# Retention and routed experts on one core: scatters of slots placed between a block's key and query scalings, seven routing groups, and logits block by block

## The chip, the cores and the metric

The kernel runs on one core of a Trainium2 chip. A core has five engines that run side by side: TensorE (PE in the profile, its weight loads PEld), VectorE (DVE), ScalarE (ACT), GpSimd (POOL) and SyncE (SP), and 16 DMA engines. The metric is the device time of one execution in microseconds (us); the median of several runs counts.

## The reference

The first half is a decaying linear attention over 4 sequences of 768 steps with 8 heads of 64. Its output is 3072 rows of 512. The second half sends each row to one of 8 experts, the one whose direction it points to most.

```
state = gamma * state + outer(k[t], v[t])        # per batch and head
x[t]  = scale * q[t] @ state                     # rows x: 3072 x 512
xn, en = x / (|x| + 1e-6), emb / (|emb| + 1e-6)
logits = xn @ en.T / tau                         # 3072 x 8
expert = argmax(logits);  gate = softmax(logits)[expert]
out[row] = gate * (relu(x[row] @ w1[expert]) @ w2[expert])
```

## The kernel before

The attention is done in 12 blocks m = 0 to 11 of 256 time steps, three to a sequence, all heads at once (loop at L773). Time inside a block is handled with products of 128 steps: keys are multiplied by gamma^-t and queries by gamma^t (scale_k L341, scale_q L334, two GpSimd instructions of 128x512 each per block), both are transposed on TensorE (L350, L368) and copied out of PSUM by ScalarE (L355, L369), then TensorE makes the scores (L381), VectorE masks them (L401), and TensorE multiplies them with the values (intra, L445) and adds the part that comes from the running state (inter, L445; the state's own products are L415). ScalarE takes the output out of the two banks py0 and py1 (take, L464 and L467). Logits of a block are one product with the experts' normalised directions (L492), which VectorE turns into rows (L500).

Blocks are scaled two ahead: in block m, GpSimd scales the keys and queries of block m+2 once the first mask of block m is done (L796 to L800, `after(..., i)`), and the transposes of block m+1 stand near the end of block m. The order of the instructions on each engine is the order in which the program is written out; nothing reorders it.

Routing goes by groups of blocks (GROUPS, L50). When a group's last block has its logits, TensorE sums them over the quarters of the features (sums, L510) and VectorE chooses the expert (choose, L520 to L530) and adds to the running counts (L548, L550). One block later TensorE counts earlier rows of the same expert (count, L537 to L541) and VectorE makes of this each row's slot in a table (ranks, L557 to L561: `sloti`). GpSimd then writes one entry per row into the table `tbl` in DRAM, by an indirect DMA for every 128 rows (place, L570): 24 of them in all, of which the first 18 are the table of the "early" rows (blocks 0 to 8). In the text a run is several such scatters one behind the other on GpSimd. In block 10 the early entries are read back (L606) and their rows gathered (L600).

In the kernel before, the scatters of block m stand behind all four scalings on GpSimd (L842): none in blocks 0 to 3, then 2, 2, 2, 3, 3, 4 in blocks 4 to 9 and the last 2 of the 18 in block 10. The directions (expert_emb, L627 to L650) are normalised in three steps at the ends of blocks 0, 1 and 2, mostly on VectorE, so logits start only in block 3, with three blocks' at once (L844). Rows of block m-1 go to DRAM with two VectorE transposes (L472) and four DMAs on SP's queue (L479); in a block with a choice they go before it, but in block 9 behind it (L857 to L870).

Behind the blocks come the experts' two layers, in which TensorE multiplies with weights split into two parts (L237, L1040, L1090). The change touches none of it.

Of the kernel before, what the change touches and what calls it, by code (L numbers as in the profile page):

```python
# [11 lines left out]
F32 = mybir.dt.float32  # L12
F32R = mybir.dt.float32r
BF16 = mybir.dt.bfloat16
FP16 = mybir.dt.float16
I32 = mybir.dt.int32
AF = mybir.ActivationFunctionType
# [7 lines left out]
P = 128  # L25
# [21 lines left out]
EROWS = ((0, P), (1, P), (2, EARLY - 2 * P))  # L47
LATE = CAPS[0] - EARLY
assert LATE == P
GROUPS = ((0, 1, 2), (3, 4, 5), (6, 7), (8,), (9, 10), (11,))  # L50
NBE = 2 * 9
SW = 16
FILL = 512
# [52 lines left out]
def retention_moe(ctx: ExitStack, tc: tile.TileContext, q, k, v, emb, tau, w1, w2, const, const16, out):  # L106
# [67 lines left out]
    def after(i, o):  # L174
        tc.add_manual_dep(i.ins, o.ins.name, SYNC, reason="pace")
# [451 lines left out]
    def expert_emb():  # L627
        em = ap_.tile([NE, DM], F32, name="parts")
        nc.scalar.dma_start(out=em, in_=emb)
        tt = cp.tile([NE, 1], F32, name="tt")  # L630
        nc.scalar.dma_start(out=tt, in_=tau.broadcast_to([NE, 1]))
        yield
        rt = cp.tile([NE, 1], F32, name="rt")
        nc.vector.reciprocal(out=rt, in_=tt)
        sq = cp.tile([P, DM], BF16, name="sq")
        es = cp.tile([NE, 1], F32, name="es")
        nc.vector.scalar_tensor_tensor(out=sq[:NE], in0=em, scalar=1.0, in1=em, op0=ALU.mult, op1=ALU.mult, accum_out=es)
        en = cp.tile([NE, 1], F32, name="en")
        steps = norm_of(en, es, NE, 1)
        next(steps)  # L640
        yield
        for _ in steps:
            pass
        nc.vector.tensor_scalar(out=em, in0=em, scalar1=en, scalar2=rt, op0=ALU.mult, op1=ALU.mult)
        yield
        ps = pt_()
        for j in range(KT):
            nc.tensor.transpose(ps[:, j * NE:(j + 1) * NE], em[:, j * P:(j + 1) * P], ident[:NE, :NE])
        nc.vector.tensor_copy(out=enT[:, :, :NE], in_=ps[:, :KT * NE].rearrange("p (j e) -> p j e", e=NE))
        yield  # L650
# [72 lines left out]
    warm = cp.tile([P, 1], F32, name="warm")  # L723
    nc.gpsimd.memset(warm, 1.0)
    nc.scalar.activation(out=warm, in_=warm, func=AF.Exp)
    make_identity(nc, ident)
    for _ in range(W0):
        nc.tensor.matmul(idle, zeros[:, :P], zeros, start=True, stop=True)
# [23 lines left out]
            turn_k(0, s, kps[s], range(2 * i, 2 * i + 2))  # L752
    copy_k(0, 0, kps[0])
    copy_k(0, 1, kps[1], nc.vector.tensor_copy)
    spread_v(0, 0)
    spread_v(0, 1)
    for s in range(2):
# [4 lines left out]

    last_of = {ms[-1]: g for g, ms in enumerate(GROUPS)}
    waiting, ready = None, []

    def place_ranks(g):
        pr = count(g)
# [5 lines left out]
    for m in range(NM):  # L773
# [8 lines left out]
        for u in range(2):  # L782
            o = masks(scores(m, u), u)
            if u == 0:
                i = o[0]
        n = 2 if m < 7 else 3 if m < 8 else 4
        if m == NM - 2:
            place(ready)
            del ready[:]
# [3 lines left out]
            nc.sync.dma_start(out=cst2, in_=const[:, _C1:])  # L793
            nc.sync.dma_start(out=tri, in_=const16)

        if m + 2 < NM:  # L796
            for s in range(2):
                after(scale_k(m + 2, s), i)
            for s in range(2):
                after(scale_q(m + 2, s), i)  # L800
        if m == 2:
            nc.gpsimd.tensor_copy(out=zt[:, :, :2].bitcast(I32), in_=C("ids").rearrange("p (n o) -> p n o", o=2))
        if m == NM - 3:
# [8 lines left out]
        if m == 0:  # L812
            state(0)
            state_copy(0)
            state_sums(0)
            intra(0, 0)
            intra(0, 1)
            transpose_k(1, 0)
# [10 lines left out]
        else:  # L829
# [9 lines left out]
                    in_=none), i)  # L839
            if waiting is not None and m < NM - 2:  # L840
                place_ranks(waiting)
            place(ready[:n])  # L842
            del ready[:n]
            for i in () if m < 3 else (0, 1, 2) if m == 3 else (m - 1,):  # L844
                logits_rows(i, logits_products(i))
            if nxt:
                state_sums(m + 1)
                spread_v(m, 1, nc.vector.tensor_copy)
                transpose_k(m + 1, 0)
                transpose_q(m + 1, 0)  # L850
                i = transpose_q(m + 1, 1)
                if m + 3 < NM:
                    after(load_v(m + 3), i)
                transpose_k(m + 1, 1)
                if m == NM - 2:
                    spread_v(m + 1, 0)
                if m == NM - 3:  # L857
                    z = sums(done)
                    run_all(choose(done, z))
                    run_all(add_counts(done))  # L860
                rows(m - 1, gathered if m == NM - 2 else None)
                if m == NM - 2:
                    for low in first:
                        low()
                    load_piece(gathered)
                    load_piece(gathered)
                if done is not None and m != NM - 3:
                    z = sums(done)
                    run_all(choose(done, z))
                    run_all(add_counts(done))  # L870
                intra(m, 0)
                intra(m, 1)
            else:
                intra(m, 0)
                z = sums(done)
                run_all(choose(done, z))
                run_all(add_counts(done))
                for low in lows:
                    low()
                intra(m, 1)  # L880
                pr = count(done)
                ps = [turn_rows(xge, EROWS, kt, bank(f"pst{kt}")) for kt in range(2)]
                run_all(ranks(done, pr))
                place(range(span(done).start, span(done).stop))
# [4 lines left out]
        if m == NM - 2:  # L889
            spread_v(m + 1, 1)  # L890
            lows = [split_cast(), split_cast()]
        if m < 3:
            next(emb_steps)
        if m == NM - 1:
            for kt in range(KT):
# [476 lines left out]
```

## Time and profile before

| what | us |
|---|---|
| median of 3 runs | 408.5 (405.87 to 409.03) |
| the profiled execution | 404.42 |
| span of its profile, first to last instruction | 402.6 |
| mean granted TensorE clock in it | 0.991 of full speed |

The page counts, for each engine, the time in which one of its instructions runs. A view of stretches cuts the span at given times; a row has start and end, the length, the busy time of PE, PEld, DVE, ACT and POOL with the number of their instructions, the granted TensorE clock as a share of full speed, the share of the DMA engines, and GB/s. The times in a timeline are from the span's start; a row ends with the idle time of its engine ahead of it and with what ended that.

### The profile page before, as it was taken

Reading aid. Unit: us, or ns where it says so; the run is one execution under the profiler, and the core shown is the slowest. Engines: PE = TensorE matmul, PEld = TensorE weight load, DVE = VectorE, ACT = ScalarE, POOL = GpSimd, SP = SyncE. Lnnn points to the kernel's source line nnn. Section 1 sums busy time; section 2 is a strip of 40 time slices with the busy share of each in tenths; the row PEclk is TensorE's granted clock in tenths of the full one; section 3 lists DMA queues with packets and bytes.
Section 4 is the critical chain, followed back from the end, with each engine's and each line's share of the span. In section 5 each row is a group of like instructions: output and inputs, shape, how many; then the busy total and the mean of one; then the engine's idle time right before and its main releaser. Section 6 shows DMA issues by size and latency. Waiting matters only on the chain.

```text
span 402.6 us, 9524 instructions
## 1 busy us (share of the span) xinstructions
PE 389.6 (97%) x3646; PEld 356.8 (89%) x3646; DVE 255.1 (63%) x539; ACT 213.4 (53%) x378; POOL 151.1 (38%) x170
## 2 busy tenths in 40 slices
PE   7999999999999999999999999999999999999992
PEld 4898888877869988999999999999889889999971
DVE  5598987667798748744861864586377446576300
ACT  4565665554784457464553845554585445453410
POOL 2677476678325252412702511340272062000131
PEclk9999999999899999999999999999999999999998
DMA  8999999888357959687878796797969887933121
GB/s 233 263 307 276 258 264 266 235 232 229 77 142 228 292 181 303 173 267 210 264 235 217 254 326 167 215 302 217 258 234 329 206 258 229 241 113 103 36 100 43
DMA packets 88479, 88.39 MB, mean 220 GB/s; under 512 B 10808, under 2 KB 67000, under 8 KB 88424
## 3 DMA queue, kind: packets, MB, share of 16 engines
q1 hardware_dynamic: 83176, 74.60, 64.9%
q0 software_dynamic: 5072, 13.03, 9.8%
q8 instruction: 30, 0.49, 0.5%
q14 instruction: 25, 0.20, 0.2%
q10 hardware_dynamic: 176, 0.07, 0.1%
HBM read 65.01 MB, written 18.79 MB: 208 GB/s over the span
## 4 chain that ended last, share of the span: by engine, by line
PE 90%; DMA 4%; issue 2%; ACT 2%; DVE 1%; SPq 1%; POOL 0%; POOLq 0%; ACTq 0%
PE pst L237 12%; PE b L237 10%; PE py L237 10%; PE py L1040 8%; PE py L445 8%; PE b L1090 6%; PE b L1040 6%; PE pst L1040 6%; PE b L381 5%; PE py L1090 4%; PE pst L415 3%; PE b L350 3%; PE pst L1090 3%; PE b L368 2%; PE b L492 1%
## 5 line engine op out<-in xcount | busy, mean ns | idle before, releaser
L224 DVE TENSOR_TENSOR wlo<-raw,whi 128x1024 fp32r<-128x1024 f32 x64 | 77.9, 1220 | 20.9 <-ACT whi L219 14.8
L1072 POOL DMA_INDIRECT out_dram<-og,si x28 | 29.1, 1038 | 126.8 <-ACT og L1065 74.9
L219 ACT CAST whi<-raw 128x1024 fp32r<-128x1024 f32 x64 | 66.2, 1043 | 3.2 <-DMA raw<-in_moe_w_dram 3.2
L1021 DVE STREAM_TRANSPOSE xt<-xg 128x384 f32<-128x384 f32 (+1 forms) x28 | 15.7, 578 | 33.6 <-DMA xg<-xs 33.5
L600 POOL DMA_INDIRECT xr<-xd,gi x24 | 29.0, 1207 | 17.2 <-DMA raw<-in_moe_w_dram 10.0
L401 DVE TENSOR_TENSOR pm<-b,mask 128x512 f32<-128x512 f32 x48 | 29.8, 681 | 8.4 <-PE b L381 8.4
L344 POOL TENSOR_TENSOR hl<-wlo,cst 128x512 f32<-128x512 f32 x22 | 22.7, 1049 | 29.9 <-DVE pm L401 13.1
L237 PE MATMUL pst<-xl,whi 128*128 128x380 f32 (+7 forms) x96 | 32.1, 335 | 0.0
L237 PE MATMUL pst<-xh,whi 128*128 128x380 f32 (+7 forms) x96 | 32.0, 334 | 0.0
L237 PE MATMUL pst<-xh,wlo 128*128 128x380 f32 (+7 forms) x96 | 32.0, 333 | 0.0
L570 POOL DMA_INDIRECT tbl<-zt,sloti x24 | 24.4, 1018 | 16.4 <-DVE sloti L561 7.3
L381 PE MATMUL b<-qT,kT 64*128 64x128 f32 x384 | 28.2, 286 | 2.4 <-DVE kT L355 0.9
L381 PEld LDWEIGHTS b<-qT,kT 64*128 64x128 f32 x384 | 24.3, 191 | 5.6 <-issue 3.3
L1022 ACT CAST xh<-xt 128x408 fp32r<-128x408 f32 (+6 forms) x28 | 14.2, 510 | 26.2 <-DVE xt L1021 25.9
L237 PE MATMUL py<-xl,whi 128*128 128x288 f32 (+7 forms) x80 | 26.3, 328 | 0.5 <-DVE xl L625 0.5
L237 PE MATMUL b<-xh,whi 128*128 128x408 f32 (+7 forms) x80 | 26.7, 334 | 0.0
L237 PE MATMUL b<-xl,whi 128*128 128x408 f32 (+7 forms) x80 | 26.7, 333 | 0.0
L237 PE MATMUL b<-xh,wlo 128*128 128x408 f32 (+7 forms) x80 | 26.6, 332 | 0.0
L237 PE MATMUL py<-xh,whi 128*128 128x288 f32 (+7 forms) x80 | 26.3, 329 | 0.0
L237 PE MATMUL py<-xh,wlo 128*128 128x288 f32 (+7 forms) x80 | 26.2, 328 | 0.0
L263 POOL TENSOR_TENSOR r<-r,half 128x4 f32<-128x4 f32 (+1 forms) x9 | 8.9, 993 | 41.7 <-DVE r L262 41.7
L445 PE MATMUL py<-pm,vs 128*64 128x128 f32 x384 | 24.5, 277 | 0.1
(222 smaller groups left out, 1032.9 us busy)
## 6 DMA issues: line engine op xcount, KB each, us to landing
raw<-in_moe_w_dram SPq DMA_DIRECT2D x60, 512.0 KB
whi<-in_q_dram SPq DMA_DIRECT2D x24, 256.0 KB
xd<-x SPq DMA_DIRECT2D x48, 128.0 KB
wlo<-in_k_dram SPq DMA_DIRECT2D x11, 512.0 KB
xs<-xr SPq DMA_DIRECT2D x6, 768.0 KB
whi<-in_v_dram SPq DMA_DIRECT2D x6, 512.0 KB
wlo<-in_v_dram SPq DMA_DIRECT2D x6, 512.0 KB
xg<-xs SPq DMA_DIRECT2D x16, 192.0 KB
```

The lines of the kernel that those rows point to most:

```text
L219: nc.scalar.copy(out=hv, in_=rv)
L224: eng.tensor_tensor(out=lv, in0=rv, in1=hv.bitcast(F32), op=ALU.subtract)
L237: nc.tensor.matmul(acc[:, :w], a[:, f], x[:, kt, cols], start=(n == 0), stop=(n == 3 * KT - 1))
L344: return eng.tensor_tensor(out=ks_r[:, m % 3, s, h], in0=kin[m % 3][:, h, s], in1=w[:, h], op=ALU.mult)
L381: nc.tensor.matmul(psc[a][:, j], kTs[m][a * D:(a + 1) * D, j, u].rearrange("p s c -> p (s c)"), q_cols(m, a, j, u), start=True, stop=True, ...
L401: o.append(nc.vector.tensor_tensor(out=pm, in0=psc[a], in1=w, op=ALU.mult))
L445: nc.tensor.matmul(pys[m][b][o * D:(o + 1) * D, j], lhsT, rhs, start=first, stop=True, skip_group_check=True)
L570: i = nc.gpsimd.indirect_dma_start(out=tbl[:, :], out_offset=bass.IndirectOffsetOnAxis(ap=sloti[:, n:n + 1], axis=0), in_=zt[:, n], in_off ...
L600: return nc.gpsimd.indirect_dma_start(out=xr[:n, j, :], out_offset=None, in_=xd[:rows_, :], in_offset=bass.IndirectOffsetOnAxis(ap=gi[:n, ...
L1040: nc.tensor.matmul(acc[:, :c], a[:, f], x[:, kt, :c], start=(n == 0), stop=(n == 3 * FT - 1))
L1072: i = nc.gpsimd.indirect_dma_start(out=out[:, :], out_offset=bass.IndirectOffsetOnAxis(ap=si[:n, e, j:j + 1], axis=0), in_=og[:n, j, :], i ...
L1090: nc.tensor.matmul(acc[:s, :], x[:, kt, at], a, start=(n == 0), stop=(n == 3 * FT - 1))
```

## The change

Seven groups instead of six, so that two groups of three become pairs and block 7 stands alone; the number of scatters per block comes from a table. On GpSimd a block's order becomes: two key scalings, scatters, two query scalings. In a block that also makes ranks (4, 6, 8, 9) one query scaling stands ahead of the scatters. In block 0 all four scalings of block 2 stand behind the steps of the directions. The directions' squares move from VectorE to ScalarE, the scaling of `emb` from VectorE to GpSimd, and the whole chain into the head and block 0. Logits are made in every block from block 1 on, one block's at a time. The choice of a group stands ahead of the rows' transposes in every block. The scatters per block become 2, 3, 2, 3, 2, 4 in blocks 4 to 9, and again 2 in block 10.

```diff
-GROUPS = ((0, 1, 2), (3, 4, 5), (6, 7), (8,), (9, 10), (11,))
+GROUPS = ((0, 1, 2), (3, 4), (5, 6), (7,), (8,), (9, 10), (11,))
+PLACES = {4: 2, 5: 3, 6: 2, 7: 3, 8: 2, 9: 4}
...
         nc.scalar.dma_start(out=tt, in_=tau.broadcast_to([NE, 1]))
         yield
+        sq = cp.tile([P, DM], BF16, name="sq")
+        es = cp.tile([NE, 1], F32, name="es")
+        nc.scalar.activation(out=sq[:NE], in_=em, func=AF.Square, accum_out=es)
+        yield
         rt = cp.tile([NE, 1], F32, name="rt")
         nc.vector.reciprocal(out=rt, in_=tt)
-        sq = cp.tile([P, DM], BF16, name="sq")
-        es = cp.tile([NE, 1], F32, name="es")
-        nc.vector.scalar_tensor_tensor(out=sq[:NE], in0=em, scalar=1.0, in1=em, op0=ALU.mult, op1=ALU.mult, accum_out=es)
...
-        nc.vector.tensor_scalar(out=em, in0=em, scalar1=en, scalar2=rt, op0=ALU.mult, op1=ALU.mult)
+        nc.gpsimd.tensor_scalar(out=em, in0=em, scalar1=en, scalar2=rt, op0=ALU.mult, op1=ALU.mult)
...
     nc.scalar.activation(out=warm, in_=warm, func=AF.Exp)
+    next(emb_steps)
...
     copy_k(0, 1, kps[1], nc.vector.tensor_copy)
+    next(emb_steps)
...
+    def scale_ahead(m, i, what=(scale_k, scale_q), ss=range(2)):
+        if m + 2 < NM:
+            for f in what:
+                for s in ss:
+                    after(f(m + 2, s), i)
...
-        n = 2 if m < 7 else 3 if m < 8 else 4
...
-        if m + 2 < NM:
-            for s in range(2):
-                after(scale_k(m + 2, s), i)
-            for s in range(2):
-                after(scale_q(m + 2, s), i)
+        if m:
+            scale_ahead(m, i, (scale_k,))
+        masked = i
...
             state_sums(0)
+            next(emb_steps)
+            scale_ahead(0, i)
...
             if waiting is not None and m < NM - 2:
                 place_ranks(waiting)
+                scale_ahead(m, masked, (scale_q,), (0,))
+            n = PLACES.get(m, 0)
             place(ready[:n])
             del ready[:n]
-            for i in () if m < 3 else (0, 1, 2) if m == 3 else (m - 1,):
-                logits_rows(i, logits_products(i))
+            scale_ahead(m, masked, (scale_q,), range(waiting is not None and m < NM - 2, 2))
+            logits_rows(m - 1, logits_products(m - 1))
...
-                if m == NM - 3:
+                if done is not None:
                     z = sums(done)
                     run_all(choose(done, z))
                     run_all(add_counts(done))
                 rows(m - 1, gathered if m == NM - 2 else None)
...
-                if done is not None and m != NM - 3:
-                    z = sums(done)
-                    run_all(choose(done, z))
-                    run_all(add_counts(done))
...
-        if m < 3:
+        if m == 0:
             next(emb_steps)
```

## Rows read from the trace of the kernel before

**Rows 1.** The page: the span and part 1.
```profile
span 402.6 us, 9524 instructions
PE 389.6 (97%) x3646; PEld 356.8 (89%) x3646; DVE 255.1 (63%) x539; ACT 213.4 (53%) x378; POOL 151.1 (38%) x170
```
**Rows 2.** Stretches from one block's first score to the next's, blocks 3 to 10.
```profile
34.38:43.34 8.96, 8.96 (x195) 7.61 (x193) 7.09 (x16) 4.66 (x9) 4.70 (x6) 1.00 1.02 293
43.34:52.14 8.80, 8.79 (x161) 7.59 (x159) 7.88 (x19) 5.67 (x10) 5.31 (x5) 1.00 0.92 256
52.14:60.71 8.57, 8.54 (x187) 7.36 (x185) 6.59 (x12) 5.47 (x10) 6.50 (x8) 1.00 0.90 253
60.71:69.22 8.51, 8.16 (x178) 7.09 (x176) 6.52 (x14) 4.89 (x9) 6.54 (x7) 1.00 0.93 258
69.22:78.46 9.24, 9.00 (x162) 7.80 (x160) 7.58 (x19) 5.11 (x9) 6.23 (x8) 1.00 0.86 241
78.46:87.87 9.41, 9.28 (x195) 7.88 (x193) 6.19 (x14) 5.49 (x10) 7.05 (x7) 1.00 0.81 230
87.87:98.16 10.29, 9.42 (x188) 7.90 (x186) 7.13 (x24) 5.48 (x10) 7.26 (x8) 1.00 0.89 229
98.16:110.89 12.73, 11.58 (x153) 9.61 (x153) 8.38 (x20) 8.01 (x13) 5.32 (x6) 0.87 0.46 112
```
**Rows 3.** The chain that ended last: start, us, what; blocks 3 and 5.
```profile
37.96 1.43 PE b L492 x24
...
41.29 0.22 PE b L510 x8
...
56.16 0.57 PE b L492 x8
```
**Rows 4.** Timeline of POOL: scatters of blocks 5, 8, 8 and 9.
```profile
60.38 0.97 POOL L570 DMA_INDIRECT tbl<-zt,sloti  x1 [0.30 <-issue]
...
85.31 1.12 POOL L570 DMA_INDIRECT tbl<-zt,sloti  x1 [0.16 <-issue]
...
88.02 0.97 POOL L570 DMA_INDIRECT tbl<-zt,sloti  x1 [0.30 <-issue]
...
99.34 0.97 POOL L570 DMA_INDIRECT tbl<-zt,sloti  x1 [0.30 <-issue]
```
**Rows 5.** Timeline of PE: the value products (intra) of block 8.
```profile
85.97 1.97 PE L445 MATMUL py<-pm,vs 128*64 128x128 f32 x32
```
**Rows 6.** Timeline of ACT: takes of blocks 5, 8, 9; a copy of keys.
```profile
61.88 1.17 ACT L467 COPY yT<-py 64x512 f32<-64x512 f32 x2 [1.59 <-PE b L381]
...
86.12 0.64 ACT L355 COPY kT<-b 128x512 f32<-128x512 f32 x1
89.75 0.58 ACT L464 COPY yT<-py 128x512 f32<-128x512 f32 x1 [2.99 <-PE b L381]
...
101.14 0.58 ACT L464 COPY yT<-py 128x512 f32<-128x512 f32 x1 [4.38 <-PE b L381]
```
**Rows 7.** A stretch in block 10, columns as in rows 2.
```profile
102.00:105.50 3.50, 3.50 (x48) 3.28 (x50) 2.92 (x7) 3.43 (x6) 1.94 (x2) 0.52 0.53 138
```
**Rows 8.** Timeline of DVE and POOL: copies of values, and a block's scalings.
```profile
57.91 1.72 DVE L394 COPY vs<-wlo 64x512 f32<-64x512 f32 x2
...
85.12 0.86 DVE L394 COPY vs<-whi 64x512 f32<-64x512 f32 x2
...
81.11 2.04 POOL L344 TENSOR_TENSOR hl<-wlo,cst 128x512 f32<-128x512 f32 x2 [1.74 <-DVE pm L401]
```
**Rows 9.** Timeline of DVE: first and last operation of block 8's choice.
```profile
87.24 0.15 DVE L520 TENSOR_REDUCE m<-b 128x4 f32<-128x32 f32 x1
...
88.58 0.17 DVE L550 TENSOR_TENSOR cum<-cum,sm 128x8 f16<-128x8 f16 x1
```
**Rows 10.** Timeline of ACT and DVE: idle time in the head and in block 0.
```profile
6.75 1.15 ACT L369 COPY qT<-b 128x512 f32<-128x512 f32 x2 [2.91 <-PE b L368]
...
18.15 0.42 DVE L428 TENSOR_TENSOR s<-pst,tB 128x256 f32<-128x256 f32 x1 [4.43 <-PE pst L415]
```

## The prediction

> **What bounds the kernel now.** I read the page first. TensorE is busy for 389.6 of 402.6 us [rows 1], so all that a reordering can win is the 13 us in which it idles, what it loses at a low clock, and what the page calls busy while it waits. Then I cut the attention at the first score of each block [rows 2]. Blocks 3 to 5 take 8.96, 8.80 and 8.57 us and TensorE is busy for all of it. Blocks 7 to 10 take 9.24, 9.41, 10.29 and 12.73, and their TensorE does no more work. So the time lies in blocks 6 to 10, and I price each against the undisturbed block at the same place in its sequence (their work has a period of three):
>
> - Block 6 against 3: block 3 makes three blocks' logits in 1.43 where one takes 0.57 [rows 3], so it would be 8.10 with one. 8.51 - 8.10 = 0.41 lost.
> - Block 9 against 3: 8.10 and two rounds of counting that block 3 lacks; each is some eight small products like the 0.22 of a sum [rows 3], an estimate of 0.5 for both. 10.29 - 8.60 = 1.69 lost.
> - Block 7 against 4: 9.24 - 8.80 = 0.44. Block 10 against 4: 12.73 - 8.80 = 3.93.
> - Block 8 against 5, less a sum of 0.22: 9.41 - 8.57 - 0.22 = 0.62.
>
> Together 7.1 us. Next I asked who comes late there, in the timelines of GpSimd, ScalarE and TensorE. The last scatter of block 5 ends at 60.38 + 0.97 = 61.35, and the take that waits for TensorE starts at 61.88, 0.53 later. In block 8 they are 88.99 and 89.75, 0.76 later; in block 9, 100.31 and 101.14, 0.83 later [rows 4, 6]. In block 8 TensorE had issued all value products by 85.97 + 1.97 = 87.94 [rows 5], and the take of their first bank, half way through them, still waited for 2.99 us [rows 6]. So results of TensorE that fall into a run of scatters are seen by ScalarE and VectorE only 0.5 to 0.8 us behind the run's end. The first scatter of a run does not show this: beside the one of 85.31 the copy of keys at 86.12 starts as soon as ScalarE is free [rows 4, 6]. The loss grows with the run, 0.4 behind a run of two and 1.7 and 3.9 behind those of three and four in blocks 8 and 9, because the next block's scores and state products then wait for takes and masks. In block 10 it costs the clock too: behind the idle stretch that the four scatters leave, the granted clock is 0.52, which is nearly all the lower level (1.2 of 2.4 GHz), for 3.5 us [rows 7], and half of that time, up to 1.75 us, is lost. These rows show a coincidence in place and size, not what holds the results.
>
> **The change part by part.**
>
> *Place of the runs.* Today a run stands behind two pairs of scalings of 2.04 each [rows 8], so it ends in the next block: block 8's starts 85.31 - 78.46 = 6.9 us into a block of 9.4 and ends at 10.5. Behind the change the key pair starts at the first mask (81.11 - 78.46 = 2.65 in) and ends 4.7 in, and a scatter takes 0.97 to 1.12 with 0.30 between [rows 4].
> Blocks 6 and 8 (two scatters): one query scaling (1.02) goes ahead, the run lies at about 5.8 to 8.2, and only its second scatter, 7.1 to 8.2, holds results. TensorE is then in the value products, which wait for none, and the take is needed 2 us later. I put 0.2 each for what they leave to blocks 7 and 9, bounded by 0 and by the 0.44 that block 5's two cost today.
> Blocks 5 and 7 (three scatters straight behind the keys): the run lies at 4.8 to 8.5. Its second and third hold results from 6.2 on, just as the last transposes are done and ScalarE has to copy queries and keys that the next scores need. Each is bounded by 0 and by 1.7, block 8's run of three today; I take 0.6, nearest to what block 7's run of three leaves to block 8 (0.62).
> Block 9 (four scatters behind one query scaling): 5.8 to 10.7, so results come at about 11.5 against 101.14 - 87.87 = 13.3 today. That is 1.8 earlier, and with a shorter idle stretch the clock need not fall (up to 1.75). Of 3.93 I leave 1.5; bounds 0.5 and 3.93.
> Block 4 loses nothing today and I leave it so. The sum: 0.2 + 0.2 + 0.6 + 0.6 + 1.5 = 3.1 against 7.1, a gain of 4.0 us.
>
> *What is queued behind.* The second query scaling of a block now waits behind its run on GpSimd and ends by about 10 in (12 in block 9). It is read by the transposes of the next block, which stand some 13 in, so 1 to 3 us of cover are left; if the run came later than that, TensorE would wait for it one for one. The next key pair wants GpSimd at 2.65 of the next block, 11.2 in, which block 9 alone crosses, where no key pair follows. The two scatters of block 10 come behind block 9's last scaling, the early table's read behind those, and the gather of rows had its place long before the transposes that read it.
>
> *A seventh group.* One more sum (0.22) and one more counting product on TensorE, all on the path: 0.3. On VectorE one more choice of 88.58 + 0.17 - 87.24 = 1.5 us [rows 9] and one more ranks of three operations; VectorE is busy for 6.2 to 7.9 us of a block of 9 [rows 2], which hides them. The choice now waits for the sums ahead of the rows' transposes: those, SP's four row writes and the loads queued behind them come 1.5 us later in four blocks. The loads are three blocks ahead, and the next masks have slack until the state products are done; bounds 0 and 1.5 (one choice) in all; I take 0, since TensorE waits for no mask of blocks 3 and 6 today.
>
> *Value copies.* A pair of them on VectorE takes 1.72 beside query scalings and 0.86 beside a scatter [rows 8]; scatters now stand beside them. TensorE's second half of the value products waits for the pair's end: bounds 0 and 0.86 gained, the difference of the two; I take 0.3, since blocks 3 to 5 show little wait [rows 2].
> The scatter beside that pair took 1.12 against 0.97 [rows 4, 8]. The Trainium skill ("SBUF - State Buffer", Who interferes with whom) says that the later of a VectorE copy in a fast mode and a GpSimd access is blocked until the other is done. By that rule runs would end up to 0.86 later and the three long ones, in blocks 5, 7 and 9, give back 3 x 0.7 = 2.1 of the gain (estimate); the row shows 0.15, and I use the row.
>
> *Directions.* ScalarE idles for 2.91 us ahead of 6.75 and VectorE for 4.43 ahead of 18.15 [rows 10]; the squares and the small chain fit into these, and the scaling of `emb` falls to GpSimd before block 2's keys have landed. Cost 0; if the experts' directions arrived late, ScalarE's queue would hold the first query copies: bounds 0 and 1.15, that pair [rows 10]. The logits of blocks 0 and 1 are made two and one blocks earlier at the same number of products: 0, bounds 0.57 either way, one block's [rows 3].
>
> Sum: -4.0 + 0.3 - 0.3 = -4.0 us. The profiled execution was 404.42, 1.8 more than its span, and lies 4.1 below the median of 408.5; I take the same gain from the median: **404.5 us**. A measurement of this kernel can tell about 1%, 4.1 us, from no change, so the forecast stands at that border.
>
> **The rivals.**
>
> *It moves the loss and does not shrink it.* If each scatter behind the first of a run stops TensorE for some 0.6 us wherever it stands, place does not matter: there are 11 such ahead of block 11 today (1, 1, 1, 2, 2, 3, 1) and 11 behind the change (1, 2, 1, 2, 1, 3, 1). Time 408.5 + 0.3, with its spread 407 to 410. For it: the runs are as long as before. Against it: equal runs of three cost 0.62 and 1.69 today.
> The Trainium skill (the same page, "SBUF: two separate sides") says that TensorE and ScalarE never wait for another engine's access to SBUF. By that rule the scatters would not be the cause at all and the time would stay, as in this rival; the trace shows the lateness but not its path.
>
> *Held results fall on the copies (slower).* In blocks 5 and 7 the runs of three now lie where ScalarE copies the next block's keys and queries. If TensorE's results stay held until 0.8 us behind the whole run, 9.3 in, then the last query copy and the key copy (0.6 each) end at 10.5 and the scores, due at 8.5, start 2 us late, twice; with block 9's loss as today and the choice held too, the sum is 2 + 2 + 0.4 + 3.93 = 8.3 and another block's choice 1.5 late, 9.8 against 7.1: 408.5 + 2.7 + 0.3 = 411.5. It decides from the point where the second scatter starts before ScalarE has seen the last transposes. For it: block 8's run held results across the gaps between its scatters [rows 4, 6]. Against it: block 7's three cost 0.62 only.
>
> *All of it goes.* If the runs end before the next block's scores wait on anything, 7.1 goes and 0.3 is added: 401.7. Against it: block 9 still has four in a row.
>
> **How the numbers follow.** Forecast (402.5 to 406.5) 0.53; loss moved, 0.23; slower, 0.14; all gone, 0.10. Faster by over 1% (below 404.4): half of the forecast's, 0.27, all of the last, 0.10, and 0.03 of the rest: 0.40. Slower by over 1% (above 412.6): most of the slower rival's upper half and some for what I don't see: 0.11. Within 1%: 0.49. The range reaches to the last rival below and the slower one above: 400.8 to 411.5.
>
> **What would show it.** Right: blocks 7 to 9 at most 9.0, 9.2 and 9.0 us and block 10 under 10.5 at full clock; takes start within 1 us of their products; scatters between the two kinds of scalings; no wait of a transpose for a scaling. Wrong: ScalarE's key and query copies of blocks 5 and 7 starting 0.5 to 0.8 behind a scatter's end and the next scores waiting for them; block 10 above 11.5; the low clock still there; or blocks 6 to 10 losing about 7 us in other places.

## The result and the profile after

The changed kernel takes 411.5 us (median of 17 runs, 408.3 to 416.8) where the kernel before takes 408.14 (17 runs, 405.87 to 410.84): a ratio of 1.0066, 95% interval 1.0042 to 1.009, so some 2.7 us more. The ratio leaves out the changed kernel's four longest executions (414.89 and more), the medians do not. The forecast was 4 us less. The profiled execution took 412.14 us, its span is 410.4; against the profiled span of before, 402.6, that is 7.8 more, a wider gap than between the medians: the profiled execution of before, 404.42, is shorter than each of its 17 runs. So a difference between the two profiles need not all be one between the kernels.

The page of the kernel after, busy time of the engines and the chain that ended last by engine, against [rows 1]:

```profile
PE 391.9 (95%) x3655; PEld 356.5 (87%) x3655; DVE 256.2 (62%) x546; ACT 214.5 (52%) x380; POOL 151.2 (37%) x171
...
PE 81%; DVE 7%; DMA 5%; issue 3%; POOL 1%; SPq 1%; ACT 0%; DVEq 0%; POOLq 0%
```

TensorE's share fell from 97 to 95%. In the chain it has 81% where it had 90, and VectorE 7% where it had 1. Cut at the first score of each block, as [rows 2] are, blocks 6 to 10 of the kernel after, and from block 11 to the first product of an expert's layer (columns as in [rows 2]):

```profile
61.41:70.92 9.51, 8.72 (x176) 7.33 (x174) 7.70 (x17) 5.47 (x10) 8.95 (x9) 1.00 0.85 233
70.92:79.82 8.90, 8.90 (x163) 7.72 (x161) 4.39 (x10) 5.42 (x10) 6.11 (x6) 1.00 0.85 242
79.82:90.11 10.29, 9.28 (x198) 7.77 (x198) 9.88 (x23) 5.47 (x10) 6.68 (x8) 1.00 0.65 174
90.11:99.41 9.30, 8.87 (x185) 7.53 (x184) 8.80 (x27) 5.57 (x10) 5.96 (x6) 1.00 0.72 193
99.41:112.15 12.74, 10.40 (x154) 8.24 (x153) 8.38 (x20) 8.01 (x13) 5.14 (x6) 1.00 0.77 184
112.15:122.75 10.60, 9.96 (x140) 6.87 (x138) 8.23 (x17) 8.39 (x15) 3.20 (x4) 1.00 0.50 126
```

and the stretch of before that answers to the last of these:

```profile
110.89:119.85 8.96, 8.89 (x139) 6.48 (x137) 8.03 (x17) 8.29 (x15) 2.43 (x3) 1.00 0.48 124
```

Blocks 6 to 10 take 50.74 us where they took 50.18 [rows 2]. Blocks 7 and 9 are shorter by 0.34 and 0.99, blocks 6 and 8 longer by 1.00 and 0.88, and block 10 is as long as it was, now at full clock but idle for 2.34. So the loss is in other blocks, and no smaller. Block 11 adds 1.64, blocks 0 to 5 add 0.67 (start of block 6 less start of block 0: 52.04 against 51.37), and the experts' part, from the first layer product on, 410.4 - 122.75 = 287.65 against 402.6 - 119.85 = 282.75, adds 4.9.

Three things stand out. First, in block 8 VectorE is busy for 9.88 of 10.29. Its timeline, GpSimd's and TensorE's there:

```profile
79.48 0.19 DVE L521 TENSOR_REDUCE m<-b 128x4 f32<-128x32 f32 x1 [2.28 <-PE py L446]
...
83.18 2.44 DVE L402 TENSOR_TENSOR pm<-b,mask 128x512 f32<-128x512 f32 x4
...
85.98 1.05 DVE L562 SCALAR_TENSOR_TENSOR sloti<-wmn,rank 128x4 int32<-128x4 f32 x1
...
89.43 1.52 DVE L526 SCALAR_TENSOR_TENSOR w<-zt,cst 128x16 f32<-128x16 f32 x1
...
85.97 1.04 POOL L340 TENSOR_TENSOR hh<-whi,cst 128x512 f32<-128x512 f32 x1
...
89.84 1.07 POOL L340 TENSOR_TENSOR hh<-whi,cst 128x512 f32<-128x512 f32 x1
...
84.48 0.64 PE L493 MATMUL b<-yT,enT 128*32 128x256 f32 x8 [0.33 <-DVE pm L402]
...
87.44 0.66 PE L351 MATMUL b<-ident,hl 128*128 128x128 f32 x4 [0.60 <-DVE parts L501]
```

The slots' sum (L562) and the choice's step (L526) take 0.16 to 0.31 us elsewhere, but for a third long one, 1.08 at 79.94. Here each ends within 0.05 us of the query scaling beside it (87.03 and 87.01; 90.95 and 90.91). The scalings stand there because the change put them behind the scatters. Such a meeting is not new in kind: the kernel before has a slots' sum of 0.84 at 74.68 that ends with a query scaling (75.52 and 75.50). New as well is that the choice (79.48 to 81.91) stands ahead of the rows' transposes. It starts 1.9 us behind the sums that it reads (77.33 + 0.27 = 77.60) and 0.6 behind the end of block 7's run (78.89), and transposes and masks queue behind it. So the first mask of block 8 starts 83.18 - 79.82 = 3.36 us into the block, 1.82 before (80.28 - 78.46), and TensorE waits for VectorE twice, 0.33 and 0.60, about the 0.88 that the block lost.

Second, the run of four still holds TensorE's results. It ends 101.12 + 0.97 - 90.11 = 12.0 us into block 9, only some 0.4 earlier than before (12.4, [rows 4]). The value products were issued by 97.22 + 1.97 = 99.19, and the take starts 3.9 us later, about 1 us behind the run's last scatter, as in [rows 4, 6]:

```profile
97.22 1.97 PE L446 MATMUL py<-pm,vs 128*64 128x128 f32 x32
...
97.00 1.26 POOL L571 DMA_INDIRECT tbl<-zt,sloti  x1 [0.16 <-issue]
...
101.12 0.97 POOL L571 DMA_INDIRECT tbl<-zt,sloti  x1 [0.30 <-issue]
...
103.07 0.58 ACT L465 COPY yT<-py 128x512 f32<-128x512 f32 x1 [5.18 <-PE b L382]
```

Third, the second expert's rows (xg) come late. Their first transpose on VectorE, the product that waits for it, and the stretch behind that wait:

```profile
163.44 1.10 DVE L1028 STREAM_TRANSPOSE xt<-xg 128x416 f32<-128x416 f32 x2 [3.53 <-DMA xg<-xs]
...
164.67 0.45 PE L238 MATMUL pst<-xh,whi 128*128 128x408 f32 x1 [2.04 <-ACT xh L1029]
...
165.00:170.00 5.00, 4.43 (x14) 3.40 (x14) 4.80 (x9) 2.51 (x5) 1.90 (x3) 0.69 0.66 243
```

That transpose starts 163.44 - 122.75 = 40.69 us behind the first layer product; before it was 36.91, and TensorE did not wait. Behind the idle 2 us the granted clock is 0.69 over 5 us, part of it at the lower level. The DMA view's row of one instruction queue (packets, MB, share), while the expert's table was loaded (136.6 to 142.5) and while its rows were (154.7 to 163.4):

```profile
q8 instruction: 1, 0.02, 1.0%
...
q8 instruction: 1, 0.02, 1.3%
```

In the kernel before the same two stretches (133.8 to 138.4, 149.9 to 156.8) have no row of that queue: there its packets come at 20 and 39 us behind the first layer product, behind both loads. An instruction packet among the loads may be chance or cause; the experiments take it up.

### The profile page after: what moved, and what is told of

The parts are those of the page before. It is cut to its first block, busy times and chain, and to the rows that moved or that the text cites. A ratio compares the mean times of both kernels' runs of the same rounds, so it can differ in the third digit from the quotient of the medians.

```text
span 410.4 us, 9557 instructions
## 1 busy us (share of the span) xinstructions
PE 391.9 (95%) x3655; PEld 356.5 (87%) x3655; DVE 256.2 (62%) x546; ACT 214.5 (52%) x380; POOL 151.2 (37%) x171
## 4 chain that ended last, share of the span: by engine, by line
PE 81%; DVE 7%; DMA 5%; issue 3%; POOL 1%; SPq 1%; ACT 0%; DVEq 0%; POOLq 0%
PE pst L238 12%; PE b L238 9%; PE py L238 9%; PE py L1047 7%; PE py L446 7%; PE b L1097 6%; PE b L1047 5%; PE b L382 5%; PE pst L1047 4%; PE py L1097 4%; PE b L351 3%; PE pst L416 2%; PE b L369 2%; DMA xg<-xs 2%; PE b L493 2%
## 5 line engine op out<-in xcount | busy, mean ns | idle before, releaser
L601 POOL DMA_INDIRECT xr<-xd,gi x24 | 30.0, 1248 | 16.3 <-ACT sq L279 9.0
L382 PE MATMUL b<-qT,kT 64*128 64x128 f32 x384 | 26.8, 281 | 3.1 <-DVE rs L558 1.3
L382 PEld LDWEIGHTS b<-qT,kT 64*128 64x128 f32 x384 | 23.4, 187 | 6.1 <-issue 2.9
L244 ACT ACTIVATE hh<-pst 128x380 fp32r<-128x380 f32 (+7 forms) x24 | 11.6, 484 | 28.3 <-PE pst L238 27.6
```

The source lines that it names most:

```text
L382: nc.tensor.matmul(psc[a][:, j], kTs[m][a * D:(a + 1) * D, j, u].rearrange("p s c -> p (s c)"), q_cols(m, a, j, u), start=True, stop=True, ...
L601: return nc.gpsimd.indirect_dma_start(out=xr[:n, j, :], out_offset=None, in_=xd[:rows_, :], in_offset=bass.IndirectOffsetOnAxis(ap=gi[:n, ...
```

## The experiments

The base of most is the head's part of the change alone, which costs nothing. Ratios are to the kernel before in the same session, with 95% intervals.

**The parts one by one.** e1: only directions in the head, block 0's scalings behind its state sums, logits per block.

> The kernel before with the head's part of the change alone: directions' chain in the head and block 0, block 0's scalings behind the state sums, logits per block. Theory 'head' (blocks 0 to 3 together are 0.5 us longer in the changed kernel, 34.52 against 34.00): the time rises by 0.5 to 1.2 us, blocks 0 to 3 end 0.5 late, and blocks 4 to 11 stay as before. Theory 'routing' (the cost comes from the order of GpSimd and the choice): within 0.3 us of before, since the head's 0.5 is taken up by waits that follow.

Measured 0.998 (0.9954 to 1.0006). The 0.5 us that blocks 0 to 3 show is no cost.

e7 adds the order to that:

```
 after(scale_k(m + 2, 0..1), i)          # as in the change
 place_ranks(waiting); after(scale_q(m + 2, 0), masked)
 place(ready[:n])                        # n and GROUPS as before
 after(scale_q(m + 2, ...), masked)
```

> The head's part and the scatters between a block's key and query scalings, nothing else (old groups and numbers of scatters, choice behind the rows). If the order is worth nothing: 0.998 of before, as the head alone. If earlier runs pay as my prediction had it: 0.990 to 0.994 (3 to 4 us less). If query scalings that run late hold VectorE's choice ('port'): 1.000 to 1.004, with instructions of the choice at 1 to 2.8 us where 0.2 is usual.

Measured 1.0013 (0.9979 to 1.0046): no gain, 1.3 us over the head alone, within the noise of the two. Block 8 of e7 and, in it, VectorE's value copies beside the scalings:

```profile
79.90:92.03 12.13, 9.75 (x195) 7.77 (x193) 7.13 (x11) 5.95 (x11) 8.82 (x9) 1.00 0.70 191
...
88.43 2.52 DVE L394 COPY vs<-whi 64x512 f32<-64x512 f32 x2
...
88.16 2.06 POOL L339 TENSOR_TENSOR hh<-whi,cst 128x512 f32<-128x512 f32 x2
```

Blocks 6, 7 and 9 of e7 are undisturbed (8.10, 8.57, 9.04), but blocks 5 and 8 take 10.22 and 12.13: an earlier run holds results inside its own block, and the value copies take 2.52 beside the two late scalings (0.86 and 1.72 in [rows 8]).

e6 adds to the head only the choice ahead of the rows (`if done is not None` in place of `if m == NM - 3`).

> The head's part and every choice ahead of the rows, nothing else (old groups, scatters behind all scalings). Theory 'choice': 1.002 to 1.005 of before, with the blocks behind a choice (5, 8) 0.4 to 1 us longer. Theory 'groups': within 0.2% of the head alone, 0.998 of before.

Measured 1.0047 (1.0014 to 1.0079), 2.7 us over the head alone. The two intervals leave 1.0 to 4.4, and the median, 407.72, is only 0.3 over that of before in the session, 407.42. In its profiled execution (span 404.3) none of blocks 5 to 8 is more than 0.1 us longer than in e1, not the 0.4 to 1 of the theory, so where the time goes was not seen.

e5 adds to the head only `GROUPS` and `PLACES`.

> The head's part and the seven groups with their places, nothing else of the change (scatters behind all scalings, choice behind the rows). Theory 'groups' (a third scatter in block 5 and one more choice are what costs: with the order undone the time stayed at 1.008 of before): 1.004 to 1.008 of before, block 6 at 9.4 or more where before has 8.51. Theory 'choice' (its place ahead of the rows costs): at most 1.001 of before, since the choice stands behind the rows here.

Measured 1.007 (1.0033 to 1.0108), 3.7 us over the head alone, the largest of the three, though its interval and e6's overlap. Blocks 6 and 8 of it:

```profile
61.96:71.85 9.89, 8.97 (x176) 7.53 (x174) 7.77 (x22) 5.48 (x10) 7.28 (x8) 1.00 0.92 247
...
80.90:90.99 10.09, 9.77 (x200) 8.18 (x198) 7.27 (x18) 5.58 (x11) 7.05 (x7) 1.00 0.76 217
```

Each follows a run of three. But block 9, behind a run of two instead of three, takes 8.61 for 10.26, and blocks 5 to 9 together 46.15 us against 45.89 in e1. That is the 0.3 that I had for a group; the rest lies elsewhere.

**The parts taken back.** e2 undoes the head's part of the change, e3 the order (all four scalings ahead of the scatters), e4 the choice's place.

> The changed kernel with the head's part undone (directions in blocks 0 to 2, logits of blocks 0 to 2 in block 3); groups, places, order and choice stay changed. Theory 'head': 0.5 to 1.2 us faster than the changed kernel, so 1.5 to 2.2 slower than before. Theory 'routing': still 2.5 to 3 us slower than before, with blocks 6, 8 and 11 as long as in the changed kernel (9.5, 10.3, 11.5).

> The changed kernel with all scatters of a block behind its four scalings again; seven groups, places, choice and head stay changed. Theory 'port' (query scalings that now run late on GpSimd hold VectorE's choice and ranks: 1.08, 1.05 and 1.52 us where 0.2 is usual): the long ones are gone, block 8 falls from 10.3 to about 9.4, the time is 1 to 2 us under the changed kernel's. Theory 'scatters hold TensorE's results wherever they stand': block 8 stays above 10, and the time stays at that of the changed kernel.

> The changed kernel with each group's choice behind the turned rows again; all else stays changed. Theory 'port': the choice comes when the query scaling is over, its long instructions fall to 0.2 us, and the time is 0.5 to 1.5 us under the changed kernel's. Rival: the choice's place costs nothing, and the time is within 0.4 us of the changed kernel's.

Measured 1.0105 (1.0068 to 1.0143), 1.0081 (1.0043 to 1.0118) and 1.0034 (1.0002 to 1.0066). Undoing the head or the order gives nothing; putting the choice back gives about 1.3 us, within the noise of the two. In e3 the long choices are gone (0.17 to 0.21) and block 8 takes 9.92, but the run of three behind the scalings makes block 6 10.02. In e4, where the rows' transposes fill the time in which the choice waits, the first mask of block 8 starts 2.1 us in (83.48 - 81.37) and the block takes 9.08, but block 6 takes 10.28. The three costs of 1.3, 2.7 and 3.7 do not add: the whole change stands 3.5 over the head alone (1.0066 - 0.998).

**What lets TensorE's results through.** e12 is e1 with a fill between the scatters of a run, of rows that nothing reads before they are gathered:

```
+    if n < 16 and n != columns[-1]:
+        nc.gpsimd.memset(xge[:, 0], 0.0)      # 128x512
```

> The head alone, with a fill of 128x512 on GpSimd (some 0.5 us, of rows that nothing reads) between the scatters of a run. Theory 'adjacent' (TensorE's results wait for a pause of the scatters): the takes start behind the first scatters, blocks 7 to 10 lose less and the time is 1 to 3 us less, 0.991 to 0.996 of before. Theory 'each scatter holds them' or 'until the last of the run': runs end 0.6 to 1.9 us later and the time is 0 to 3 us more than the head alone's, 0.998 to 1.005.

Measured 0.9935 (0.9911 to 0.9958). First e1: the value products of block 7, its takes, its run, and blocks 7 and 8:

```profile
79.29 1.97 PE L445 MATMUL py<-pm,vs 128*64 128x128 f32 x32
...
81.20 0.59 ACT L464 COPY yT<-py 128x512 f32<-128x512 f32 x1 [0.93 <-PE py L445]
82.75 1.17 ACT L467 COPY yT<-py 64x512 f32<-64x512 f32 x2 [0.96 <-PE b L381]
...
78.38 1.01 POOL L570 DMA_INDIRECT tbl<-zt,sloti  x1 [0.30 <-DVE sloti L561]
79.70 0.97 POOL L570 DMA_INDIRECT tbl<-zt,sloti  x1 [0.30 <-issue]
80.98 0.97 POOL L570 DMA_INDIRECT tbl<-zt,sloti  x1 [0.30 <-issue]
...
71.91:81.19 9.28, 8.99 (x161) 7.79 (x160) 7.50 (x19) 5.11 (x9) 6.47 (x8) 1.00 0.84 239
81.19:90.48 9.29, 9.21 (x194) 7.80 (x192) 6.19 (x14) 5.48 (x10) 6.91 (x7) 1.00 0.81 228
```

and the same of e12:

```profile
76.86 1.97 PE L445 MATMUL py<-pm,vs 128*64 128x128 f32 x32
...
78.00 0.59 ACT L464 COPY yT<-py 128x512 f32<-128x512 f32 x1 [0.15 <-PE py L445]
78.91 1.17 ACT L467 COPY yT<-py 64x512 f32<-64x512 f32 x2 [0.33 <-PE py L445]
...
76.57 1.01 POOL L570 DMA_INDIRECT tbl<-zt,sloti  x1 [0.16 <-issue]
77.59 0.54 POOL L574 MEMSET xge<- 128x512 f32 x1
78.30 0.97 POOL L570 DMA_INDIRECT tbl<-zt,sloti  x1 [0.17 <-issue]
...
79.97 0.97 POOL L570 DMA_INDIRECT tbl<-zt,sloti  x1 [0.16 <-issue]
...
70.19:78.76 8.57, 8.57 (x162) 7.61 (x160) 7.53 (x20) 5.70 (x10) 6.82 (x8) 1.00 1.05 288
78.76:87.39 8.63, 8.63 (x194) 7.65 (x192) 6.33 (x13) 5.48 (x10) 8.11 (x10) 1.00 0.90 244
```

In e1 the products were issued by 81.26, and the second take starts at 82.75, 0.8 us behind the run's end (81.95); the first starts inside the run, but late as well. In e12 the products were issued by 78.83 and the second take starts at 78.91, in the middle of a scatter, although the run ends no sooner behind its start; blocks 7 and 8 lose nothing. The kernel before has 9.24 and 9.41 for these two blocks [rows 2], as e1 has. So neither the number of scatters nor their place holds the results, but that they follow each other without a pause. Block 11 gives some of it back: 10.35, 8.92 in e1.

e16 has a fill of 128x8 in the same place.

> The head alone with a fill of 128x8 (some 0.1 us) between the scatters of a run where the run before had one of 128x512 (0.54 us). If any instruction between two scatters lets TensorE's results through: 0.991 to 0.996 of before, blocks 6 to 8 at 8.1, 8.6 and 8.6. If it is the length of the pause that counts: 0.996 to 1.000, blocks 7 and 8 at 9.2 to 9.3 as in the head alone.

```profile
77.04 1.01 POOL L570 DMA_INDIRECT tbl<-zt,sloti  x1 [0.30 <-DVE sloti L561]
78.05 0.29 POOL L574 MEMSET xge<- 128x8 f32 x1
78.35 0.97 POOL L570 DMA_INDIRECT tbl<-zt,sloti  x1
```

Measured 0.9999 (0.9967 to 1.003); blocks 7 and 8 take 9.03 and 9.38. The short fill goes into the 0.30 us that stood between two scatters anyway: they start 1.31 apart, as without it (1.32), and 1.73 apart in e12. It is the pause that counts, 0.7 us against 0.30, not an instruction in between. In all these runs the longer pause holds a fill; an idle one was not run.

e11 is e1 with two scatters in block 9 and the other two in block 10 (`n = 2 if m < 7 or m == 9 ...`); e14 has that, the fills, and fills between the scatters of block 10 and the three early gathers too.

> The head alone, with two scatters in block 9 where it has four, and the other two with those of block 10. Theory 'run' (TensorE loses what a long run holds): block 10, 15.65 in the profile of the head alone and 12.73 before, falls to 9.5 to 11, the next block gets some of it, and the time is 1 to 4 us less, 0.988 to 0.996 of before. Theory 'each scatter costs wherever it stands': within 0.3% of the head alone.

> The head alone with fills between scatters, now also between those of block 10 and between the three gathers of the early rows, and two scatters in block 9 instead of four. Theory 'adjacent': blocks 9 to 11, 10.12, 11.16 and 10.35 with fills alone, fall by 1 to 2 us together, and the time is 0.989 to 0.993 of before. Rival (what is left there is not the scatters'): 0.992 to 0.996, as with fills alone.

Measured 0.9997 (0.9974 to 1.0021) and 0.9935 (0.991 to 0.9959). e11 does not decide between its theories: GpSimd has nothing to do between the two places, so in its profile the four scatters still follow each other (one ends at 98.73, the next starts at 99.04). It shows only that the place in the program is worth nothing. In e14, too, no fill stands between the two pairs (96.74 and 97.04), and there the take of block 9 starts 1.5 us behind its products (98.52 and 97.03), where e12 has 0.2 (97.23 and 97.05). In time the further fills gave nothing over e12.

**The choice beside the scalings.** e8 is the changed kernel with one operand in PSUM:

```
- scalar_tensor_tensor(out=w, in0=zd[:, r], scalar=0.0, in1=C("e16"), op0=is_lt, op1=add)
+ tensor_tensor(out=z, in0=z, in1=bc(m), op=is_lt)      # z in PSUM
+ tensor_tensor(out=z, in0=z, in1=C("e16"), op=add)
- tensor_reduce(out=rank[:, r], in_=rs, ...)
+ tensor_reduce(out=pr[:, 448:448 + nb], in_=rs, ...)   # read by the slots' sum
```

> The changed kernel, but the choice's step that adds the expert's number, the comparison behind it and the slot's sum read one operand from PSUM, so that none of them reads two operands from SBUF; one VectorE instruction more per group. Theory 'port' (an operation with two SBUF inputs waits for a GpSimd scaling to end): the long instructions of blocks 7 and 8 (1.08, 1.05, 1.52) fall to 0.2 to 0.4 us, block 8 falls from 10.3 to 9.4, and the time is 0.8 to 2 us under the changed kernel's. Rival (the length has another cause, or VectorE has slack there): the time is within 0.5 us of the changed kernel's.

Measured 1.0038 (1.0 to 1.0076), 1.1 us under the changed kernel, within the noise of the two. The slots' sum that ran beside the scaling of 88.73 to 89.77:

```profile
88.89 0.16 DVE L564 SCALAR_TENSOR_TENSOR sloti<-wmn,b 128x4 int32<-128x4 f32 x1
...
88.73 1.04 POOL L340 TENSOR_TENSOR hh<-whi,cst 128x512 f32<-128x512 f32 x1
```

The lengths are settled: 0.16 beside a scaling. TensorE's two waits for VectorE in block 8 are gone, but the block took 10.36 and did not fall to 9.4: in this profile the run of block 7 ends 1.6 us into it (84.07 - 82.48), and block 7's take comes at 84.04, 2.4 behind its products.

**Instruction packets among the second expert's loads.** e9 is e1 with `W0 = 10` idle products replaced by 8 and 18 narrow ones; e10 and e13 are the changed kernel with 2 and 36, and 6 and 34.

> The head alone (0.998 of before), with the 10 idle products of TensorE's warm-up replaced by 8 of the same and 18 narrow ones of 64 columns: 32 more instructions on TensorE and no other work. Theory 'code' (in all six profiles with seven groups a 16 KB instruction packet comes at 16.7 to 17.3 and at 35.6 to 38.4 us behind the first layer product, among the packets of the expert's table and of its rows, and in all four with six groups it comes at 19 to 21 and 39 to 40, behind both): the packets move to about 17 and 37, the first transpose of the second expert's rows starts at 38.8 or later behind the first product instead of 37 to 38, and the time rises to 1.002 to 1.007 of before without any of the change's routing. Theory 'groups' (the extra group's own work costs): 0.996 to 1.000 of before.

Measured 1.0045 (1.0011 to 1.0078), apart from e1's interval, with none of the change's routing. Its packets came at 16.9 and 37.8 us as forecast, the rows' transpose 162.16 - 120.54 = 41.62 behind the first product:

```profile
162.16 1.11 DVE L1027 STREAM_TRANSPOSE xt<-xg 128x416 f32<-128x416 f32 x2 [2.95 <-DMA xg<-xs]
...
163.39 0.45 PE L237 MATMUL pst<-xh,whi 128*128 128x408 f32 x1 [1.46 <-ACT xh L1028]
```

> The changed kernel, with the 10 idle products replaced by 2 of the same and 36 narrow ones: 56 more instructions on TensorE. Theory 'code': the instruction packets move to some 11 to 12 and 31 us, between the two small loads, the second expert's first transpose starts at 37 to 38, and the time is 1 to 3 us under the changed kernel's, 1.000 to 1.004 of before. Theory 'groups': the changed kernel's time, 1.006 to 1.008 of before.

> The changed kernel with its 10 idle products replaced by 6 of the same and 34 narrow ones (60 more instructions on TensorE, which stays busy to about 5.8 us as in the changed kernel). The run before this moved the instruction packets as meant and the second expert's rows came in time, but its median did not fall; it left TensorE idle for 1.6 us in the head. Theory 'code': packets at about 13 and 30 us behind the first layer product, the second expert's first transpose at 38 to 38.6 behind it, and the time 1 to 2.5 us under the changed kernel's, 1.001 to 1.004 of before. Rival (the lateness of the rows is a small part, and other losses fill it): 1.006 or more, as the changed kernel.

In both the packets left the two loads (13.0 and 30.2; 12.6 and 30.0) and the transpose came at 38.41 and 38.91 where the changed kernel has 40.69, in time. Yet they took 1.0128 (1.0089 to 1.0167) and 1.0103 (1.007 to 1.0136). So more instructions on TensorE's queue move these packets, and 32 of them alone cost e9 time: that is shown. That the packets make the rows late is not. In e15, e17 and e18 below, too, a packet falls into the load of the table (16.7, 15.9 and 16.5 us behind the first product), yet from the issue of that load to the first gather that reads it pass 4.48, 4.89 and 4.78 us, 4.59 in the kernel before, 5.84 in the changed kernel and 7.20 in e9. Their rows come in time, at 37.50, 36.78 and 37.27, ahead of the second packet. So a packet among the table's bytes does not by itself delay them, and what does is open. Nor do late rows explain the changed kernel's time: in e13 other places lose (block 10 takes 14.06), and why is open.

**The changed kernel with fills.** e15 is the changed kernel with e12's fill, e18 that with e8's operands; e17 is e5 with the fill.

> The changed kernel with a fill of 128x512 on GpSimd between the scatters of a run. Theory 'adjacent': it gains what the head alone gained, 0.4 to 0.5%, and stands at 1.000 to 1.004 of before; what is left over the head with fills (0.9935) is the late rows of the second expert and the choice that meets query scalings. Rival (the order between key and query scalings already shortens the runs, so fills only delay the query scalings): 1.005 to 1.010.

Measured 1.0107 (1.0079 to 1.0135): no gain. The fills do here what they do in e12: the first takes of blocks 5 to 9 start at most 0.2 us behind their products, up to 3.9 in the changed kernel. But the query scalings end later still, five choices and slot sums take 1.00 to 1.52, a comparison beside a scaling takes 2.50, and block 11 takes 13.52.

> The head's part, seven groups with their places, and fills of 128x512 between the scatters of a run (scatters behind all scalings, choice behind the rows). If seven groups cost only by their longer runs: the fills take that away, 0.991 to 0.996 of before, as with six groups. If they cost by the instruction packets among the second expert's loads: 0.998 to 1.002, with the first transpose of its rows 38.8 us or more behind the first layer product.

> The changed kernel with the fills and with the choice's and ranks' operations reading one operand from PSUM. With fills alone the changed kernel stood at 1.0107 of before, and five such operations took 1.00 to 1.52 us. Theory 'port': without these waits the time falls by 1 to 3 us, to 1.003 to 1.008. Rival (the late query scalings cost in another way, or the order itself does): 1.008 to 1.013.

These two ran on a chip on which the kernel before takes 401.59 us, some 6 less than elsewhere; they took 404.94 and 405.82, ratios 1.0103 (1.0057 to 1.0149) and 1.0128 (1.0082 to 1.0175). What the fills and the operands gain elsewhere they don't tell. Both theories of e17 missed: its ratio lies above either range, and its rows came in time. Their profiles show two waits. In e17's block 6 the slots' sum ends with the query scalings (67.50 and 67.47), and TensorE stands behind it:

```profile
65.66 1.84 DVE L562 SCALAR_TENSOR_TENSOR sloti<-wmn,rank 128x4 int32<-128x4 f32 x1
...
65.42 2.05 POOL L340 TENSOR_TENSOR hh<-whi,cst 128x512 f32<-128x512 f32 x2
...
67.92 0.66 PE L351 MATMUL b<-ident,hl 128*128 128x128 f32 x4 [0.71 <-DVE parts L501]
```

In e18 blocks 6 to 10 take 44.19 us (50.18 before), and then TensorE waits for the early gathers, which hang on the scatters of block 10:

```profile
113.85 0.33 PE L622 MATMUL pst<-ident,xge 128*128 128x128 f32 x1 [1.19 <-DMA xge<-xd,tb]
...
105.55:118.19 12.64, 10.81 (x140) 7.11 (x138) 10.39 (x24) 8.40 (x15) 6.27 (x7) 0.84 0.30 72
```

Block 11 takes 12.64 for 8.96 before, with the clock at 0.84: 3.7 of the 6 us are given back there.

## Why the prediction was wrong

**What bounds it** was read rightly: TensorE, with losses in the blocks behind runs of scatters. That the runs cause them was only a coincidence in the rows; e12 shows it. Not every held result waits for the end of its run, though: the first take of e1's block 7 starts inside it (81.20).

**Place of the runs** is the step that failed. It let the loss shrink from 7.1 to 3.1 us because runs end earlier in their block. By the same measure blocks 6 to 10 of the changed kernel lose 1.41, 0.10, 1.50, 0.70 and 3.94, together 7.65, where it had 0.6, 0.2, 0.6, 0.2 and 1.5. Of blocks 7 to 10, forecast at 9.0, 9.2, 9.0 and under 10.5 at most, only block 7 (8.90) came out so; the others took 10.29, 9.30 and 12.74.

Two things in it were wrong. The runs do not end as early as it had them: key scalings were to start 2.65 us into a block and start 3.94, 4.15 and 3.68 into blocks 5, 8 and 9, whose runs end 9.7, 10.0 and 12.0 in, not 8.5, 8.2 and 10.7. And place is not what matters: the order alone gained nothing (e7). What matters is the pause between two scatters (e12, e16), which the change leaves at 0.30. So the largest term, the run of four, of whose 3.93 it left 1.5, still costs 3.94, at full clock; the take behind it starts 103.07 - 90.11 = 13.0 us into its block, where 13.3 was before and 11.5 the forecast.

The rival that moves the loss had this right, but not the time (407 to 410), since in the profile the other blocks and the experts' part were longer too. The slower rival gave the measured median, 411.5, by luck. Its main mechanism did not occur: block 5's key and query copies ran on time (58.17 to 60.28), and it was the take that waited for its run's end, as before. Its side term, a choice held by a run, did, in block 7 (79.48).

**A seventh group** was put at 0.3. In the blocks it is that (46.15 against 45.89); alone it measured 3.7. So the cost lies outside what the term counted. The second expert's rows are late in e5 too, at 39.43, as e9 makes them late without a group, but TensorE waits only 0.36 for them there. Where most of the 3.7 goes, and what makes the rows late, is open.

**The choice ahead of the rows** was put at 0, bounds 0 and 1.5, since the next masks were to have slack. Alone it measured 2.7, with 1.0 to 4.4 in the noise, so that it costs is shown, that it costs more than the bound is not. In block 8 of the changed kernel the slack was gone: behind the held choice the first mask came 1.5 us later, and TensorE waited 0.93 for VectorE.

**What is queued behind** asked who reads the query scalings (TensorE's transposes, which indeed did not wait) and not what runs beside them on VectorE. The Trainium skill ("SBUF - State Buffer", SBUF: two separate sides) has it: a VectorE operation with two SBUF inputs and a GpSimd operation that reads SBUF lock each other out for the whole instruction. The trace agrees (1.52 and 1.84 us where 0.2 is usual, ending with the scaling; 0.16 with one operand in PSUM). I had weighed only its rule on copies. The same section's rule that TensorE and ScalarE never wait for another engine's access stood for the reading that the scatters are no cause at all; e12 speaks against that reading, and by what path the results are held no run shows.

**Value copies** took 0.86 to 1.02 in blocks 4 to 9, as forecast, but TensorE had not waited for them, so nothing came of it. **Directions and logits** at 0 were right: 0.998. **The clock** did not fall in block 10 of the profiled execution, as forecast, but the block took 12.74 at full clock; in eleven of the eighteen experiments' profiles it fell there again (0.66 to 0.68 over the block in e1, e5 and e7). It did not in the five with the fills of 128x512, but neither in e4 and e6, which have none, and in e15, e17 and e18 it fell in block 11 (0.75 to 0.84).

The fastest versions are e12 and e14, the head's part and the pauses without the change's routing, at the same ratio; e12 takes 404.33 us where the kernel before has 407.23 in the same session, 2.6 us less by the ratio.

## What to carry to other kernels

Before moving a disturbing run, ask what in it disturbs: with the head's part alone, half a microsecond of other work between two scatters gained what no place for the run did. Beside the rest of the change the same fills gained nothing (e15), so a remedy counts only in the kernel that it was measured in. When work is moved on one engine, list what will run beside it on the other engines, not only who reads its result. And price a change's small instruction counts over the whole kernel with runs of the part alone: with 32 more instructions in the head a load came late more than a hundred microseconds behind them, for a reason that stands nowhere in the diff.

## What the runs showed of the hardware

- With 0.30 us between two indirect DMAs on GpSimd, results of TensorE reached ScalarE late, mostly 0.4 to 1.1 us behind the end of the run (82.75 for products issued by 81.26 in e1; 103.07 for 99.19 in the changed kernel). With 0.7 us between them, filled with a memset, they were seen within 0.1 us in the middle of a scatter (78.91 for 78.83 in e12). By what path is not shown.
- A VectorE operation with two operands in SBUF ended with the GpSimd scaling beside it (0.84 to 2.50 us where 0.2 is usual); with one operand in PSUM it took 0.16 (e8).
- 32 more instructions on TensorE in the head moved 16 KB instruction packets by 2 to 4 us, more than a hundred microseconds later, and the rows' first reader started 41.62 us behind the first product (e9), against 37.95 (e1). In e15 a packet fell among the table's bytes too, and the reader started at 37.50.
- One chip ran the same kernel before in 401.59 us where five other sessions had 406.62 to 408.14.
